# A fused attention and channel-mix kernel: a reworked head, and a tanh whose planned dependency is one half of its PSUM bank

## The chip, the cores and the metric

The kernel runs on one core of a Trainium2 chip. The core has TensorE (matmuls and, beside them, weight loads), VectorE (DVE), ScalarE (ACT), GpSimd (POOL) and SyncE (SP), each with a queue of its own that is worked in order, and 16 DMA engines. The metric is the device time of one execution in microseconds (us). The kernel before takes 528.45 us, the median of three runs (527.47 to 528.96).

## The reference, cut to what matters

```python
# q, k, v: [B, N, C] = [4, 6208, 256] float32; tau = 1.0
qn = q / (norm(q, axis=1) + 1e-6);  kn = k / (norm(k, axis=1) + 1e-6)
a  = softmax(kn.transpose(0, 2, 1) @ qn / tau)      # [B, 256, 256], over the last axis
x  = v @ a                                          # [B, N, 256]
x_prev = x shifted by one row along N, zeros first
xk = mu_k * x + (1 - mu_k) * x_prev;  xr = mu_r * x + (1 - mu_r) * x_prev
k  = maximum(xk @ w_k, 0)                           # w_k: [256, 1024]
v  = (k * k) @ w_v                                  # w_v: [1024, 256]
out = v / (1 + exp(-(xr @ w_r)))                    # w_r: [256, 256]
```

## The kernel before, in words

**Batches and blocks.** Each batch has 6208 = 12 x 512 + 64 rows. For each batch the kernel needs first a covariance of k with q over all rows and the norms of their columns, then a softmax that gives the 256 x 256 matrix A, and then works through the rows in blocks of 512 (the four rests of 64 rows make one block together, 49 blocks in all). While the blocks of one batch are worked, the covariance of the next is gathered, group by group (lines 615 to 665).

**One block.** The rows of v are turned so that rows lie along the free axis (DMA transposes from line 341, for the first five blocks transposes on TensorE at line 351, copied out of PSUM by DVE at line 353). x is A times the turned v (line 427) and is copied out of PSUM by ScalarE (437; for the first block half by DVE, 434). DVE makes the differences of neighbouring rows and the two mixes xk and xr (467, 475, 484). "Up" (513) multiplies xk with w_k in four pairs of 512-wide results in the PSUM tiles kT0 and kT1; ScalarE takes the relu (516) and DVE squares it (518). Then, for each of the block's four tiles of 128 rows, one of two PSUM banks vr0, vr1 is used: the **gate** (546) writes xr times w_r to the right half `V[:, D:]`, and four **down** steps (551), each of two matmuls, gather the product with w_v in the left half `V[:, :D]`. ScalarE takes the **tanh** (555) of the right half, and DVE (557) adds one, multiplies with the left half and writes the result tile. The bank of a tile is used again two tiles later.

**The head.** Batch 0 has nothing to lie beside. SP loads q and k in float32, 512 KB at a time, into a ring of ten tiles (280), DVE casts them to bf16 (291) into eight tiles for q (q0) and three for k (k0); ScalarE, for every second k DVE (297), squares them (300) into a ring of three tiles (s0). TensorE adds the covariance (313) and the column sums of the squares (306 for q into vr1, 319 for k into vr0). The short group 12 (64 rows) is loaded between groups 5 and 6 of k. Then come the q norms (lines 236 to 267, with a power on POOL at 239), a softmax chain over DVE, POOL and ScalarE (365 to 393), x, the mixes and the first up. Loads of v, of the weights and of the next batch's q and k are issued by POOL, and these DMAs cast to bf16 on their way (335, 673 to 681, 622).

**What sets the order.** All of this is given to a planner (`Plan`, lines 24 to 101). `add(engine, duration, key, function, reads, writes)` enters a step; the names in reads and writes are the planner's own and make its dependencies. `order()` plans each engine's steps: a step is ready when its predecessors end plus a fixed lag (0.3 us towards TensorE, 0.12 to ScalarE and DVE, 0.15 to POOL, 0.02 on the same engine), and of the ready steps that with the lowest key starts. The instructions are then emitted in the order of planned start, and that order is each engine's program order. The plan's times are not known to the chip: what an instruction waits for there is worked out anew by the framework, from the tiles that the emitted instructions touch, in the order in which they were emitted. A dependency given by `after=` alone exists in the plan only; before the change the loads of v and of the weights are held in this way behind the planned cast of k's group 10.

Of the kernel before, what the change touches and what calls it, by code (L numbers as in the profile page):

```python
# [113 lines left out]
def dve(n, mode=1):  # L114
    return 0.16 + n / 960 / mode
# [3 lines left out]
def kernel(  # L119
# [13 lines left out]
    nc = tc.nc  # L133
    B, N, C = q.shape
    D = C
# [18 lines left out]
    def ring(name, n, shape, dt=BF16):  # L154
        return [sbuf(f"{name}{i}", shape, dt) for i in range(n)]
# [9 lines left out]
    w_r = sbuf("w_r", [2, D])  # L165
    A = [sbuf(f"A{b}", [2, C]) for b in range(B)]

    NF, NQ0, NK0 = 10, 8, 3
    f32s = ring("f32s", NF, [S, C], F32)
    q0 = ring("q0", NQ0, [S, C])  # L170
    k0 = ring("k0", NK0, [S, C])
    s0 = ring("s0", 3, [S, C])
    sq = ring("sq", 2, [2, S, C])
    t1 = ring("t1", 2, [2, 2, C])
    t2 = ring("t2", 2, [2, C])
# [96 lines left out]
    for i, (tn, g, j0, j1) in enumerate(order0):  # L272
        key = H0 + i
        t = q if tn == "q" else k
        rows = P if g < NB else L
        fs = fslot % NF
        fslot += 1
        f = f32s[fs]
        n = j1 - j0
        add("SP", 0.45, key, lambda f=f, t=t, g=g, j0=j0, j1=j1, rows=rows: nc.sync.dma_start(  # L280
            f[:rows, j0:j1], src(t, 0, g)[:, j0:j1, :]), writes=[("f", fs)], size=rows * n * C * 4, name="ld0")
        if tn == "q":
            ci = g % NQ0
            cast, cres = q0[ci], ("q0", ci)
        else:
            ci = g % NK0
            cast, cres = k0[ci], ("k0", ci, j0)
        wr = [cres]
        if tn == "k" and j0 == 0:
            wr = [("k0", ci, 0), ("k0", ci, 2), ("k0", ci, 3)] if g != NB - 1 else [("k0", ci, 0)]  # L290
        add("DVE", dve(n * C, 2), key, lambda f=f, cast=cast, j0=j0, j1=j1, rows=rows: nc.vector.tensor_copy(
            cast[:rows, j0:j1], f[:rows, j0:j1]), reads=[("f", fs)], writes=wr, name="cast0")
        si = nsq % 3
        nsq += 1
        s2 = s0[si]
        if tn == "k" and g < NB - 1 and g % 2 == 1:
            add("DVE", dve(n * C, 2), key + 0.5, lambda s2=s2, cast=cast, j0=j0, j1=j1, rows=rows: nc.vector.tensor_tensor(
                s2[:rows, j0:j1], cast[:rows, j0:j1], cast[:rows, j0:j1], op=OP.mult), reads=[cres], writes=[("s0", si)], name="sq0")
        else:
            add("ACT", act(n * C), key, lambda s2=s2, f=f, j0=j0, j1=j1, rows=rows: nc.scalar.activation(  # L300
                s2[:rows, j0:j1], f[:rows, j0:j1], AF.Square), reads=[("f", fs)], writes=[("s0", si)], name="sq0")
        if tn == "q":
            for j in range(j0, j1):
                def go(s2=s2, j=j, rows=rows, st=(i == 0 and j == 0)):
                    for ih in range(2):
                        nc.tensor.matmul(vr[1][:, ih:ih + 1], s2[:rows, j, ih * P:(ih + 1) * P], ones[:rows, 0:1],
                                         start=st and ih == 0, stop=False, skip_group_check=True)
                add("PE", 0.13, key + 0.3, go, reads=[("s0", si)], writes=[("vr", 1)], name="nq0")
        else:
            for j in range(j0, j1):  # L310
                def go(ci=ci, g=g, j=j, rows=rows):
                    for ih in range(2):
                        nc.tensor.matmul(s_ps[:, ih, :], k0[ci][:rows, j, ih * P:(ih + 1) * P], q0[g % NQ0][:rows, j],
                                         start=g == 0 and j == 0 and ih == 0, stop=False, skip_group_check=True)
                add("PE", 2 * pe(C), key + 0.1, go, reads=[cres, ("q0", g % NQ0)], writes=[("s_ps",)], name="cov0")

                def go(s2=s2, j=j, rows=rows, st=(g == 0 and j == 0)):
                    for ih in range(2):
                        nc.tensor.matmul(vr[0][:, ih:ih + 1], s2[:rows, j, ih * P:(ih + 1) * P], ones[:rows, 0:1],
                                         start=st and ih == 0, stop=False, skip_group_check=True)  # L320
                add("PE", 0.16, key + 0.2, go, reads=[("s0", si)], writes=[("vr", 0)], name="nk0")
        if tn == "q" and g == NB:
            kq = key + 0.6
            add("DVE", dve(2), kq, lambda: nc.vector.tensor_copy(nrm[0][:, 0:2], vr[1][:, 0:2]),
                reads=[("vr", 1)], writes=[("nq", 0)], name="rq")
            inverse(0, kq, nrm[0], "nq", 0, 2, "rq")
            spread(0, kq, "rq")
# [17 lines left out]
    def v_turn_pe(n, key, pb, other=None):  # L345
        i, o = n % NV, n % NT
        tp = pb[0]

        def go():
            for j in range(2 * S):  # L350
                nc.tensor.transpose(tp[:, j * P:(j + 1) * P], v_bf[i][:, j // 2, (j % 2) * P:(j % 2 + 1) * P], ident)
        add("PE", 8 * 0.06, key, go, reads=[("v_bf", i)], writes=[pb[1]] + ([other] if other else []), name="turn v")
        add("DVE", dve(2 * M, 2), key + 0.1, lambda: nc.vector.tensor_copy(vT[o].rearrange("p a b -> p (a b)"), tp),
            reads=[pb[1]], writes=[("vT", o)], name="turn v")

# [50 lines left out]
    def x_stage(n, key):  # L406
# [11 lines left out]
        for ci, (c0, c1) in enumerate(cuts):  # L418
            for dh in range(2):
                kx = key + dh * (.3 * T if n else .01) + ci * .05  # L420

                dst = xp[:, c0:c1] if n else kT[0][:, dh, c0:c1]
                dres = ("xp",) if n else ("kT", 0, dh)

                def go(dh=dh, c0=c0, c1=c1, dst=dst):
                    for ih in range(2):
                        nc.tensor.matmul(dst, A[b][:, ih, dh * P:(dh + 1) * P],  # L427
                                         vT[o].rearrange("p (s h) q -> p h s q", h=2)[:, ih, c0 // P:c1 // P, :],
                                         start=ih == 0, stop=ih == 1)

                def both(go=go, kx=kx, w=c1 - c0, dh=dh, c0=c0, c1=c1, dst=dst, dres=dres):
                    add("PE", 2 * pe(w), kx, go, reads=[("A", b, 0), ("A", b, 1), ("vT", o)], writes=[dres], name="x")
                    if n == 0 and dh == 1:
                        add("DVE", dve(w), kx, lambda: nc.vector.tensor_copy(xR[:, dh, at + c0:at + c1], dst),
                            reads=[dres], writes=[("x", i, dh)], name="x evac")
                    else:
                        add("ACT", act(w), kx, lambda: nc.scalar.copy(xR[:, dh, at + c0:at + c1], dst),  # L437
                            reads=[dres], writes=[("x", i, dh)], name="x evac")
                unit(kx, both)

    def mix_stage(n, key):
# [93 lines left out]
    def down_tile(n, s, kd, last):  # L535
# [3 lines left out]
        def go():  # L539
# [4 lines left out]
            def gate():  # L544
                for dh in range(2):
                    nc.tensor.matmul(V[:, D:], xr[ri][:, dh, s * P:(s + 1) * P], w_r[:, dh, :], start=dh == 0, stop=dh == 1)  # L546
            add("PE", 2 * pe(D), kd, gate, reads=[("xr", ri), ("w_r",)], writes=[("vr", bk)], name="gate")
            for p in range(4):
                def dn(p=p):
                    for fh in (2 * p, 2 * p + 1):  # L550
                        nc.tensor.matmul(V[:, :D], kk[n % 2][:, fh, s * P:(s + 1) * P], w_v[:, fh, :], start=fh == 0, stop=fh == 7)  # L551
                c0 = (256 if s * P >= 256 else 0) if n == 0 else 0
                add("PE", 2 * pe(D), kd + .01 * p, dn, reads=[("kk", n % 2, p, c0), ("w_v",)], writes=[("vr", bk)], name="down")
            r = res[oi]
            add("ACT", act(D), kd + .3, lambda: nc.scalar.activation(r[:, s], V[:, D:], AF.Tanh, scale=0.5),  # L555
                reads=[("vr", bk)], writes=[("res", oi, s)], name="tanh")
            add("DVE", 0.15 + D / 960, kd + .4, lambda: nc.vector.scalar_tensor_tensor(  # L557
                r[:, s], r[:, s], 1.0, V[:, :D], op0=OP.add, op1=OP.mult), reads=[("vr", bk)], writes=[("res", oi, s)], name="out")
            if last:
# [53 lines left out]
    def cov_group(b, g, key, dk):  # L613
# [12 lines left out]
        def work():  # L626
# [28 lines left out]
            def go():  # L655
                for x in range(4):
                    nc.tensor.matmul(xp[:, x:x + 1], cols[x], ones[:rows, 0:1], start=x == 0, stop=x == 3,
                                     skip_group_check=True)
            add("PE", 0.3, kn, go, reads=[wres], writes=[("xp",)], name="norm")
            ai = b % 2  # L660
            if g == 0:
                add("DVE", dve(4), kn + .1, lambda: nc.vector.tensor_copy(acc[ai], xp[:, 0:4]), reads=[("xp",)], writes=[("acc", ai)], name="norm")
# [4 lines left out]
        unit(key, work)  # L667


    gate_w = [s for s in cast_done if s.name == "cast0"][-4:-3]  # L670
    gate_qk = gate_w
    v_load(0, KC - 2, after=gate_w)
    add("POOL", 0.75, KC - 1.9, lambda: nc.gpsimd.dma_start(w_k, moe_w_k.rearrange("(ko ki) f -> ki ko f", ki=P)),
        writes=[("w_k",)], size=D * DF * 4, name="ld w", after=gate_w)
# [13 lines left out]
    add("PE", 0.3, KC + .01, go, reads=[("mu_rows", 0), ("mu_rows", 1)], writes=[("vr", 1)], name="mu")  # L688
    add("DVE", dve(4), KC + .01, lambda: nc.vector.tensor_copy(mu, vr[1][:, 0:4]), reads=[("vr", 1)], writes=[("mu",)], name="mu")
    tps = [kT[1][:, 0, :].bitcast(BF16), kT[1][:, 1, :].bitcast(BF16)]  # L690
    v_turn_pe(0, KC + .02, (tps[0], ("kT", 1, 0)))
    v_turn_pe(1, KC + .5, (tps[1], ("kT", 1, 1)))

    NPE = 5
    for n in range(2, NPE):
# [34 lines left out]
        fn()  # L730
    seq = plan.order()
    tc_plan[:] = seq
    for s in seq:
        s.fn()


# [36 lines left out]
```

## Time and profile before

| what | value |
|---|---|
| median of three runs | 528.45 us |
| the profiled execution, its own time | 527.72 us |
| its span in the trace | 526.0 us |
| DVE busy | 417.8 us (79%) |
| ScalarE busy | 398.5 us (76%) |
| L551 down matmuls, 1552 of them | 273 ns each, one tile uses eight |
| L555 tanh, 194 of them | 387 ns each |
| L557 result on DVE, 194 of them | 417 ns each |
| L516 relu, 200 of them | 1001 ns each |
| L634 squares of the next batch on ScalarE, 39 of them | 1816 ns each |

The span is the time from the first to the last instruction that the profile shows; the rest of the execution's own time lies around it. Matmuls are pipelined, so two of 273 ns that follow each other at once are shown as 0.38 us together, and TensorE's busy time is that of overlapping instructions counted once. "PE" stands for TensorE's matmuls, "PEld" for its weight loads. In a list of instructions, x2 stands for two instructions merged into one line. A bracket at the end of a line holds the idle time of the engine before the instruction and what ended it.

### The profile page before, as it was taken

The page shows a single profiled execution, that of the slowest core. Times are in us where ns is not written, and L with a number is a line of the kernel's source. Part 1 is how long each engine was busy: PE and PEld are TensorE (multiplying, and loading weights), DVE is VectorE, ACT ScalarE, POOL GpSimd, SP SyncE. Part 2 cuts the span into 40 slices and gives each one's busy share as a digit, 9 for nine tenths or more (in the row PEclk, how much of TensorE's full clock was granted, in tenths as well). Part 3 has the DMA queues.
Part 4 walks back from the last instruction along what each step waited for, and adds up shares of the span by engine and source line. Part 5 has one row for each costly group of instructions (what it writes and reads, how often), then busy time and mean ns, then how long its engine had stood idle before and what let it go on. Part 6 is the DMA issues. An engine that isn't in the chain of part 4 may idle for free.

```text
span 526.0 us, 9943 instructions
## 1 busy us (share of the span) xinstructions
PE 491.1 (93%) x3707; PEld 342.7 (65%) x3761; DVE 417.8 (79%) x970; ACT 398.5 (76%) x573; POOL 88.7 (17%) x148
## 2 busy tenths in 40 slices
PE   1785999999899999999999999999999999999996
PEld 1563777756567767666667776666666666666674
DVE  4565997788879877798888778798888887878873
ACT  6543999788789978877898868877776787777763
POOL 0054433331123233211111210010010100000000
PEclk9998999999999999999999999999999999999999
DMA  8999999999999999998758854556465563413123
GB/s 333 402 312 206 205 187 203 197 203 206 212 191 133 205 188 161 210 215 128 127 106 145 147 90 92 126 102 145 97 99 143 105 143 81 121 40 102 41 81 100
DMA packets 113944, 83.23 MB, mean 158 GB/s; under 512 B 49572, under 2 KB 101352, under 8 KB 113896
## 3 DMA queue, kind: packets, MB, share of 16 engines
q0 software_dynamic: 38160, 33.01, 43.1%
q1 hardware_dynamic: 75736, 49.59, 36.5%
q8 instruction: 29, 0.48, 0.4%
q14 instruction: 19, 0.16, 0.1%
HBM read 78.71 MB, written 25.43 MB: 198 GB/s over the span
## 4 chain that ended last, share of the span: by engine, by line
PE 77%; DVE 7%; DMA 7%; issue 4%; ACT 3%; POOL 2%; SPq 0%; ACTq 0%; POOLq 0%
PE vr L551 28%; PE kT L513 28%; PE vr L546 7%; PE xp L427 6%; PE s_ps L650 6%; DMA f32s<-in_q_dram 3%; ACT kr L516 2%; DMA f32s<-in_k_dram 2%; DMA vT<-v_bf 2%; DVE kk L518 2%; DVE dm L475 1%; DVE res L557 1%; DVE dl L467 1%; DVE xk L484 1%; POOL v_bf L335 1%
## 5 line engine op out<-in xcount | busy, mean ns | idle before, releaser
L551 PE MATMUL vr<-w_v,kk 128*128 128x256 bf16 x1552 | 251.3, 273 | 1.0
L516 ACT ACTIVATE kr<-kT 128x1024 bf16<-128x1024 f32 (+1 forms) x200 | 198.6, 1001 | 53.2 <-PE kT L513 48.3
L513 PE MATMUL kT<-xk,w_k 128*128 128x512 bf16 (+1 forms) x746 | 213.4, 372 | 7.5 <-DVE xk L484 4.5
L551 PEld LDWEIGHTS <-kk 128*128 128x128 bf16 x1552 | 149.2, 98 | 83.8 <-issue 0.4
L518 DVE TENSOR_TENSOR kk<-kr 128x1024 bf16<-128x1024 bf16 (+1 forms) x200 | 134.7, 674 | 49.2 <-ACT kr L516 47.2
L555 ACT ACTIVATE res<-vr 128x256 f32<-128x256 f32 x194 | 74.1, 387 | 37.6 <-PE vr L551 35.1
L513 PEld LDWEIGHTS <-w_k 128*128 128x128 bf16 x800 | 77.6, 98 | 33.3 <-issue 5.0
L557 DVE SCALAR_TENSOR_TENSOR res<-res,vr 128x256 f32<-128x256 f32 x194 | 80.4, 417 | 18.2 <-ACT res L555 17.2
L546 PE MATMUL vr<-w_r,xr 128*128 128x256 bf16 x388 | 72.7, 272 | 2.5 <-DVE res L557 2.2
L634 ACT ACTIVATE sq<-f32s 128x2048 bf16<-128x2048 bf16 (+1 forms) x39 | 70.8, 1816 | 0.0
L335 POOL DMA_DIRECT2D v_bf<-in_v_dram x48 | 36.8, 766 | 197.4 <-DMA vT<-v_bf 170.3
L475 DVE TENSOR_SCALAR dm<-dl,mu 128x512 bf16<-128x512 bf16 (+1 forms) x200 | 62.4, 349 | 0.6
L437 ACT CAST xR<-xp 128x512 bf16<-128x512 f32 x94 | 55.3, 589 | 7.7 <-PE xp L427 7.2
L427 PE MATMUL xp<-vT,A 128*128 128x512 bf16 x188 | 56.9, 385 | 0.1
L546 PEld LDWEIGHTS <-xr 128*128 128x128 bf16 x388 | 37.7, 98 | 19.7 <-issue 3.8
L650 PE MATMUL s_ps<-f32s 128*128 128x256 bf16 (+1 forms) x294 | 48.8, 272 | 0.1
L467 DVE TENSOR_TENSOR dl<-xR 128x1024 bf16<-128x1024 bf16 (+1 forms) x49 | 33.1, 677 | 9.2 <-ACT xR L437 9.2
L300 ACT ACTIVATE s<-f32s 128x1024 bf16<-128x1024 f32 (+3 forms) x23 | 21.1, 926 | 18.3 <-DMA f32s<-in_q_dram 9.1
L622 POOL DMA_DIRECT2D f32s<-in_q_dram x39 | 21.1, 541 | 74.0 <-ACT res L555 15.1
L484 DVE TENSOR_TENSOR xk<-dm,xR 128x1024 bf16<-128x1024 bf16 (+1 forms) x49 | 33.2, 678 | 0.3
L484 DVE TENSOR_TENSOR xr<-dm,xR 128x1024 bf16<-128x1024 bf16 (+1 forms) x49 | 33.2, 677 | 0.3
L650 PEld LDWEIGHTS <-f32s 128*128 128x128 bf16 (+1 forms) x294 | 28.0, 97 | 4.7 <-issue 0.6
(68 smaller groups left out, 237.5 us busy)
## 6 DMA issues: line engine op xcount, KB each, us to landing
out_dram<-res SPq DMA_DIRECT2D x47, 512.0 KB, 3.7
v_bf<-in_v_dram POOLq DMA_DIRECT2D x48, 256.0 KB, 6.6
f32s<-in_q_dram POOLq DMA_DIRECT2D x36, 256.0 KB, 9.6
f32s<-in_k_dram POOLq DMA_DIRECT2D x36, 256.0 KB, 9.8
f32s<-in_q_dram SPq DMA_DIRECT2D x12, 512.0 KB, 7.7
f32s<-in_k_dram SPq DMA_DIRECT2D x11, 512.0 KB, 9.5
vT<-v_bf SPq DMA_TRANSPOSE x43, 3.9
w_k<-in_moe_w_k_dram POOLq DMA_DIRECT2D x1, 512.0 KB, 8.6
```

Of the source, the lines that this page charges most:

```text
L427: nc.tensor.matmul(dst, A[b][:, ih, dh * P:(dh + 1) * P], vT[o].rearrange("p (s h) q -> p h s q", h=2)[:, ih, c0 // P:c1 // P, :], start=i ...
L475: unit(km, lambda col=col, dh=dh, c0=c0, c1=c1, km=km, w=w: add("DVE", dve(w, 4), km, lambda: nc.vector.tensor_scalar_mul(dm[di][:, dh, c0 ...
L484: nc.vector.tensor_tensor(o[which][:, :, c0:c1], dm[di][:, :, c0:c1], xR[:, :, at + c0:at + c1], op=OP.add)
L513: nc.tensor.matmul(kT[bk][:, x, :w], w_k[:, dh, fh * P:(fh + 1) * P], xk[n % 2][:, dh, c0:c1], start=dh == 0, stop=dh == 1)
L516: add("ACT", act(2 * w), ku + .1, lambda: nc.scalar.activation(kr[kri][:, :, :w], kT[bk][:, :, :w], AF.Relu, scale=0.5 ** 0.5), reads=[("k ...
L518: add("DVE", dve(2 * w, 2), ku + .2, lambda: nc.vector.tensor_tensor(kk[n % 2][:, 2 * p:2 * p + 2, c0:c1], kr[kri][:, :, :w], kr[kri][:, : ...
L546: nc.tensor.matmul(V[:, D:], xr[ri][:, dh, s * P:(s + 1) * P], w_r[:, dh, :], start=dh == 0, stop=dh == 1)
L551: nc.tensor.matmul(V[:, :D], kk[n % 2][:, fh, s * P:(s + 1) * P], w_v[:, fh, :], start=fh == 0, stop=fh == 7)
L555: add("ACT", act(D), kd + .3, lambda: nc.scalar.activation(r[:, s], V[:, D:], AF.Tanh, scale=0.5), reads=[("vr", bk)], writes=[("res", oi, ...
L557: add("DVE", 0.15 + D / 960, kd + .4, lambda: nc.vector.scalar_tensor_tensor(r[:, s], r[:, s], 1.0, V[:, :D], op0=OP.add, op1=OP.mult), re ...
L634: add("ACT", act(w), key, lambda: nc.scalar.activation(Q[:rows, :, :n], G[:rows, :, :n], AF.Square), reads=both, writes=[("sq", si)], name ...
L650: nc.tensor.matmul(s_ps[:, ih, :], G[:rows, 1, s, ih * P:(ih + 1) * P], G[:rows, 0, s, :], start=g == 0 and s == 0 and ih == 0, stop=g == ...
```

## The change

The change edits two places.

In the **head**: the ring for squares s0 grows from three to six tiles and that for k from three to five. The planned costs of the norm steps on TensorE fall (0.13 and 0.16 to 0.06, in later batches 0.3 to 0.15). The loads that POOL issues are no longer held in the plan only: a small copy on POOL reads the cast of k's group 9, and all loads are planned after it; since it is an instruction of POOL's queue, what is emitted behind it on POOL runs behind it. The first two turned blocks of v are copied out of PSUM by ScalarE and no longer by DVE, with other keys. The planner's resource for the first block's x is split into two column halves, so that the plan no longer holds the second quarter's matmuls behind the first one's copy. Last, "fillers": between the last norm step of k and the first gate, matmuls with no use are emitted into the right half of vr1, as many as fill 0.8 of each gap that the plan shows on TensorE.

In the **tiles of every block**: the gate writes a planner's resource of its own, `("vr", bk, "g")`, and the tanh reads that alone and is entered ahead of the down steps. So in the plan the tanh depends on the gate and no longer on the four down steps. The gate in turn depends on the last down step of the tile before in its bank, and no longer on DVE's read of that tile.

```diff
-    NF, NQ0, NK0 = 10, 8, 3
+    NF, NQ0, NK0 = 10, 8, 5
-    s0 = ring("s0", 3, [S, C])
+    s0 = ring("s0", 6, [S, C])
...
-        si = nsq % 3
+        si = nsq % 6
...
-                add("PE", 0.13, key + 0.3, go, reads=[("s0", si)], writes=[("vr", 1)], name="nq0")
+                add("PE", 0.06, key + 0.3, go, reads=[("s0", si)], writes=[("vr", 1)], name="nq0")
...
-                add("PE", 0.16, key + 0.2, go, reads=[("s0", si)], writes=[("vr", 0)], name="nk0")
+                add("PE", 0.06, key + 0.2, go, reads=[("s0", si)], writes=[("vr", 0)], name="nk0")
...
+        if n < 2:
+            add("ACT", 1.03, key + 0.1, lambda: nc.scalar.copy(vT[o].rearrange("p a b -> p (a b)"), tp),
+                reads=[pb[1]], writes=[("vT", o)], name="turn v")
+            return
...
-                dres = ("xp",) if n else ("kT", 0, dh)
+                dres = [("xp",)] if n else [("kT", 0, dh), ("kT", 0, dh, c0)]
...
-                    add("PE", 2 * pe(w), kx, go, reads=[("A", b, 0), ("A", b, 1), ("vT", o)], writes=[dres], name="x")
+                    add("PE", 2 * pe(w), kx, go, reads=[("A", b, 0), ("A", b, 1), ("vT", o)] + (dres[:1] if n == 0 else []), writes=dres[-1:], name="x")
...
-            add("PE", 2 * pe(D), kd, gate, reads=[("xr", ri), ("w_r",)], writes=[("vr", bk)], name="gate")
+            add("PE", 2 * pe(D), kd, gate, reads=[("xr", ri), ("w_r",), ("down", bk)], writes=[("vr", bk, "g")], name="gate")
+            r = res[oi]
+            add("ACT", act(D), kd + .3, lambda: nc.scalar.activation(r[:, s], V[:, D:], AF.Tanh, scale=0.5),
+                reads=[("vr", bk, "g")], writes=[("res", oi, s)], name="tanh")
             for p in range(4):
...
-                add("PE", 2 * pe(D), kd + .01 * p, dn, reads=[("kk", n % 2, p, c0), ("w_v",)], writes=[("vr", bk)], name="down")
-            r = res[oi]
-            add("ACT", act(D), kd + .3, lambda: nc.scalar.activation(r[:, s], V[:, D:], AF.Tanh, scale=0.5),
-                reads=[("vr", bk)], writes=[("res", oi, s)], name="tanh")
+                add("PE", 2 * pe(D), kd + .01 * p, dn, reads=[("kk", n % 2, p, c0), ("w_v",)], writes=[("vr", bk), ("down", bk)], name="down")
...
-    gate_w = [s for s in cast_done if s.name == "cast0"][-4:-3]
-    gate_qk = gate_w
+    gate = sbuf("gate", [1])
+    gate_qk = gate_w = [add("POOL", 0.3, KC - 3, lambda: nc.gpsimd.tensor_copy(gate, k0[(NB - 3) % NK0][:, 0, 0:1]),
+                            reads=[("k0", (NB - 3) % NK0, 0)], writes=[("gate",)], name="gate")]
...
-    v_turn_pe(0, KC + .02, (tps[0], ("kT", 1, 0)))
-    v_turn_pe(1, KC + .5, (tps[1], ("kT", 1, 1)))
+    v_turn_pe(0, KC - .02, (tps[0], ("kT", 1, 0)))
+    v_turn_pe(1, KC + .36, (tps[1], ("kT", 1, 1)))
...
+    fill_from = max(s.start for s in seq if s.name == "nk0")
+    fill_to = min(s.start for s in seq if s.name == "gate" and s.eng == "PE")
+    free = None
     for s in seq:
+        if s.eng == "PE":
+            if free is not None and fill_from < s.start <= fill_to:
+                for _ in range(int(0.8 * (s.start - free) / pe(C))):
+                    nc.tensor.matmul(vr[1][:, C:], ident, q0[0][:, 0], start=True, stop=True)
+            free = s.start + s.dur
         s.fn()
```

More of the change, by code (lines that the diff above doesn't have):

```diff
@@ L431, in both @@
                 def both(go=go, kx=kx, w=c1 - c0, dh=dh, c0=c0, c1=c1, dst=dst, dres=dres):
-                    add("PE", 2 * pe(w), kx, go, reads=[("A", b, 0), ("A", b, 1), ("vT", o)], writes=[dres], name="x")
+                    add("PE", 2 * pe(w), kx, go, reads=[("A", b, 0), ("A", b, 1), ("vT", o)] + (dres[:1] if n == 0 else []), writes=dres[-1:], name="x")
                     if n == 0 and dh == 1:
                         add("DVE", dve(w), kx, lambda: nc.vector.tensor_copy(xR[:, dh, at + c0:at + c1], dst),
-                            reads=[dres], writes=[("x", i, dh)], name="x evac")
+                            reads=dres, writes=[("x", i, dh)], name="x evac")
                     else:
                         add("ACT", act(w), kx, lambda: nc.scalar.copy(xR[:, dh, at + c0:at + c1], dst),
-                            reads=[dres], writes=[("x", i, dh)], name="x evac")
+                            reads=dres, writes=[("x", i, dh)], name="x evac")
                 unit(kx, both)
@@ L658, in go @@
                                      skip_group_check=True)
-            add("PE", 0.3, kn, go, reads=[wres], writes=[("xp",)], name="norm")
+            add("PE", 0.15, kn, go, reads=[wres], writes=[("xp",)], name="norm")
             ai = b % 2
```

## The prediction

> **What bounds the kernel now.** I read the page first, then the busy time by windows, then the list of waits, then the timeline of the head (0 to 62 us) and of a stretch in the middle.
>
> ```profile
> span 526.0 us, 9943 instructions
> PE 491.1 (93%) x3707; PEld 342.7 (65%) x3761; DVE 417.8 (79%) x970; ACT 398.5 (76%) x573; POOL 88.7 (17%) x148
> PE   1785999999899999999999999999999999999996
> ```
>
> TensorE is busy in 93% of the span, and its row of tenths is 9 from the fifth slice on. The windows say it more sharply:
>
> ```profile
> 40.00:50.00 10.00, 6.10 (x54) 3.55 (x51) 4.52 (x14) 3.15 (x10) 5.20 (x9) 0.83 1.27 205
> 200.00:300.00 100.00, 98.74 (x730) 68.24 (x738) 83.28 (x197) 83.97 (x120) 18.73 (x30) 1.00 0.89 157
> 400.00:500.00 100.00, 99.17 (x676) 67.21 (x690) 83.07 (x188) 74.34 (x118) 3.70 (x6) 1.00 0.40 94
> ```
>
> The first number after the length is TensorE's busy time: 1.3 us idle between 200 and 300, 0.8 between 400 and 500. So TensorE sets the end; a microsecond it loses anywhere after 62 us is lost for the whole. The head (to about 57 us) is a chain of another kind: loads, then TensorE at half rate, then the softmax chain.
>
> **The tanh (the large part).** Three rows of the waits show how the program guards the banks of vr:
>
> ```profile
> ACT res L555 <- PE vr L551: 35.1, 53, 2.2
> ACT s L300 <- PE vr L319: 7.4, 4, 2.9
> PE vr L546 <- DVE res L557: 2.2, 5, 0.7
> ```
>
> L555 is the tanh, which reads only the gate's half of the bank; yet 53 times ScalarE sat idle until a down matmul (L551, the other half) had ended. The third row is the reverse case, and decides: the gate (L546) writes the right half and waits for the DVE step (L557) that reads the left half. So whatever the planner notes of halves, the built program orders all accesses to a bank as they are emitted, a TensorE write behind a read of the other half too.
>
> The emission order is the planned start. Before, the tanh depended on the last of four down steps. After, it is ready 0.12 us after the gate in the plan, and is planned as soon as ScalarE is free; every down step emitted later than it must then wait for it, on TensorE, with all of TensorE's queue behind. The middle of the run shows what that meets:
>
> ```profile
> 301.01 1.05 ACT L516 ACTIVATE kr<-kT 128x1024 bf16<-128x1024 f32 x1
> 301.42 0.38 PE L546 MATMUL vr<-w_r,xr 128*128 128x256 bf16 x2
> 301.86 0.38 PE L551 MATMUL vr<-w_v,kk 128*128 128x256 bf16 x2
> ...
> 302.30 0.38 PE L551 MATMUL vr<-w_v,kk 128*128 128x256 bf16 x2
> ...
> 302.73 0.38 PE L551 MATMUL vr<-w_v,kk 128*128 128x256 bf16 x2
> ...
> 303.17 0.38 PE L551 MATMUL vr<-w_v,kk 128*128 128x256 bf16 x2
> ...
> 303.59 0.38 ACT L555 ACTIVATE res<-vr 128x256 f32<-128x256 f32 x1 [1.53 <-PE vr L551]
> ```
>
> Columns: start, duration, engine, line. The gate starts at 301.42, the four down steps follow 0.44 apart with covariance matmuls between, and ScalarE is free from 302.06. The new tanh goes there, behind the down step of 301.86 and before that of 302.30.
>
> Price of one such tanh: the step before it ends 0.38 after its start; the tanh starts 0.04 later (303.17 + 0.38 = 303.55, tanh at 303.59), takes 0.38, and the release of TensorE takes about 0.05 (at 47.84 a DVE step ends, at 47.88 L427 starts). Sum 0.85 from one down step to the next, instead of 0.44: a stall of 0.41. I went through the timeline tile by tile in this way, ScalarE's other work left where it is. In 149 of 194 tiles ScalarE comes free between the gate and the last down step; the stall there is 0.41 us in the mean (mean spacing of down steps 0.47). 149 x 0.41 = **61 us**. The other 45 tiles keep the tanh behind the downs, at nothing.
>
> Bounds: below, half the tiles (97) at 0.25 us, as the planner's ScalarE is fuller than the chip's and as other TensorE work may sit beside the wait: 24 us. Above, all 194 at 0.61 (down steps back to back, 0.24 apart, as at 306.64 with 0.60 for four matmuls): 118 us. The five existing waits of L546 (2.2 us, 0.44 each) are the nearest row of one bank wait on TensorE, and they agree with 0.41. Gains of the earlier tanh: DVE's step L557 waited 17.2 us for it, but DVE is not the bound. In the last two tiles the two tanhs behind the last down (0.82 us at 521.60) come off the end: about -0.4 us.
>
> The Trainium skill, "PSUM — Partial Sum Buffer", section "PSUM bank collisions raise a hardware error", says that two engines on one bank and quadrant collide even at different columns and that PSUM is to be guarded by bank. By a rule of addresses this edit would cost nothing and gain the -0.4; by the page's rule the stalls stand.
>
> **The head, step by step.**
> *Six tiles for squares, five for k.* ScalarE waited 7.4 us for the k-norm matmuls (L319), since three s tiles were full; the cast of k at 32.18 waited for L313. The last piece of k is issued at 29.4 and takes 7.8 us to land, so 37.2; the last covariance starts at 40.8, so TensorE is late, not the loads. Four covariance and four norm steps take 2.05 us per group while matmuls start 0.21 apart, and 1.07 us after 36.2 where they start 0.11 apart. From 29.35 on 7.3 groups are open (5 to 11 and the short one). If TensorE, no longer interrupted, speeds up 3.4 us earlier (the low stretch of the clock later, 46.5 to 49.9, is as long): 3.5 us slow are 1.7 groups, 5.6 x 1.07 follow, end at 38.8. If not, 6.9 us slow are 3.4 groups, end at 40.4. Now it is 41.0. I take -1.5 us, between the two; bounds -3.6 (the loads) and 0.
> *Cast loads behind a copy of k on POOL.* The first load of v was issued at 30.77; now POOL waits for the cast of group 9, issued at 24.9 and, with the 9 us of its kind, landed near 33.9. Behind it queue all of POOL's issues: v, w_k, w_r, w_v, q and k of the next batch, later the softmax's pow. Head loads land up to 1 us earlier (33.9 plus two groups at 1.27, the pitch of the early issues, is 36.4). The first v (6.6 to 9.7 us from issue to landing) comes at 41 to 44, needed turned for x at about 43. I take 0: the transfers keep their total, and the lower figure suffices; bounds -1 and +3.
> *Turned v on ScalarE.* DVE's two copies (L353, 0.68 and 0.67) delay the norm copy by 0.5 (42.0 to 42.52) and the second A by 0.5 (45.25 to 45.76): -1.0 us. ScalarE's copy (nearest row: 0.59 for 512 elements, 1.02 for 1024) lies in ScalarE's idle 2.4 us before the exponentials; if not, it costs its 1.0: bounds -1.0 and +1.0.
> *x by quarter banks.* The plan no longer holds the second quarter, but the bank order above does (L427 at 47.88 waited for L434): 0.
> *Fillers.* TensorE's mean clock is 0.63 and 0.52 in the windows 46 to 48 and 48 to 50. Kept warm, eight x matmuls on the path start 0.11 instead of 0.21 apart: -0.6. The filler number follows planned gaps at 0.8; an overrun holds the chain a few tenths: bounds -1 and +1.
> Lower planned costs of norm steps only reorder: 0.
>
> The skill's "TensorE: Matmul & The Clock Gate", Part 1, gives about 3.4 us of activity for full clock and the same idle for half. It agrees with that record, but its section "A second HAM failure mode: psum-queue depth-cycling" says that frequent short idles around PSUM banks throttle too. By that the tanh stalls would cost clock as well, which no row here shows.
>
> Head: -1.5 + 0 - 1.0 + 0 - 0.6 = -3.1 us.
>
> **Sum.** The profiled execution took 527.72 us (span 526.0 plus 1.7 outside), 0.1% under the median 528.45. 527.7 + 61 - 0.4 - 3.1 = 585.2, on the median's scale 0.7 more: **586 us**.
>
> **Rivals.**
> *The tanh stays behind the downs.* ScalarE's planned queue is so full that tanhs come after the last down step, as 45 tiles already do; or the bank wait is not built for this pair. Then only the head counts: 528.4 - 3.5 = 524.9, faster. For: ScalarE is 84% busy at 200 to 300. Against: 53 tanhs ended an idle time of ScalarE. It decides below about 9 tiles with a stall (3.5 / 0.41). Chance 0.10.
> *The head gives nothing and few tanhs stall* (under 4 us together): within 0.3% of 528.4. Chance 0.03.
> *The stalls feed on themselves.* A tanh that waits in ScalarE's strict order also holds the relu behind it, so squares and the next downs come late; every tile pays the upper price: 528.4 + 118 - 3.5 = 643. If the clock falls to half in stretches as well, it is more: at 50 to 60 us TensorE was busy 8.1 of 10 us with clock 1.00, which speaks against that. Chance 0.12.
> *Main case,* 550 to 620 around 586: 0.75.
>
> **How the numbers follow.** The predicted time is the main case. The range leaves out the faster side (0.13 with the unchanged case) and some of the upper rival: 548 (24 us of stalls, less 4) to 635, short of the upper rival's 643. 0.3%, 1.6 us, is about what a measurement here can tell from no change. Slower: 0.75 + 0.12 = 0.87; same 0.03; faster 0.10.
>
> **What would show it.** Right: a wait of L551 for the tanh line on ScalarE near 150 times and some 60 us in all, TensorE idle about 12% in 200 to 300, ScalarE's wait for L551 much below 35.1. The head: first full up matmuls about 3 us earlier, clock 1.00 from 40 to 50. Wrong: tanhs that start only after the fourth down step, or TensorE still 98% busy there; then the first rival holds. A first v landing after 42 would show the POOL hold.

## The result and the profile after

| kernel | median (range), us | ratio to before, 95% interval |
|---|---|---|
| before | 528.7 | |
| changed | 557.8 (555.0 to 560.6) | 1.0555 (1.0499 to 1.0612) |

The changed kernel is 29 us slower, half of the loss that was forecast (586 us, range 548 to 635). The profiled execution took 557.28 us with a span of 555.5, 29.5 more than before. The page of the changed kernel:

```profile
span 555.5 us, 10169 instructions
PE 516.6 (93%) x3815; PEld 348.4 (63%) x3815; DVE 416.9 (75%) x968; ACT 403.8 (73%) x575; POOL 90.2 (16%) x149
L558 PE MATMUL vr<-w_v,kk 128*128 128x256 bf16 x1552 | 259.6, 272 | 15.1 <-ACT res L553 11.8
L558 PEld LDWEIGHTS <-kk 128*128 128x128 bf16 x1552 | 149.5, 97 | 112.7 <-issue 39.2
L561 DVE SCALAR_TENSOR_TENSOR res<-res,vr 128x256 f32<-128x256 f32 x194 | 81.0, 418 | 74.0 <-PE vr L550 32.1
```

The lines have moved: down is L558, gate L550, tanh L553, the result step L561. TensorE's share stays 93% and its busy time *grows* by 25.5 us with the same products. The 54 fillers (L745) add some 6 us of that, and up to 12 come from records: of the 800 up matmuls before, the trace holds 746. The rest is that a busy time of matmuls hides short stalls: a matmul that is not followed at once shows its full 272 ns, while one that is followed at once adds only about 0.11 us. The weight loads do not hide them. Their idle time in front of downs that is put to "issue" (no released wait of their own; they stand behind the matmul that waits) went from 0.4 to 39.2 us, and the tanh's line appears as a releaser of downs. The waits of the changed kernel:

```profile
ACT res L553 <- PE vr L558: 45.5, 98, 0.9
PEld L558 <- issue: 39.2, 110, 0.9
DVE res L561 <- PE vr L550: 32.1, 35, 1.8
...
PE vr L558 <- ACT res L553: 11.8, 42, 0.8
```

The second half of each step is in its timeline:

```profile
301.43 1.04 PE L558 MATMUL vr<-w_v,kk 128*128 128x256 bf16 x8
...
302.30 0.38 PE L654 MATMUL s_ps<-f32s 128*128 128x256 bf16 x2
...
302.50 0.38 ACT L553 ACTIVATE res<-vr 128x256 f32<-128x256 f32 x1 [0.23 <-PE vr L558]
...
302.94 0.38 PE L558 MATMUL vr<-w_v,kk 128*128 128x256 bf16 x2 [0.25 <-ACT res L553]
```

The last of the eight down matmuls ends at 302.47, the tanh starts 0.03 later, ends at 302.88, and the next down starts 0.06 behind it, though TensorE could have gone on at 302.52.

To add such gaps up, I take for every matmul after 60 us the time to the next start, less its own streaming time (0.11 us for 256 columns, 0.216 for 512), and book what is over 0.06 us to the line that starts late; such sums are called **gaps** below. Before: 4.4 us in front of downs (22 times), 4.3 of gates. Changed: **33.9 in front of downs (122 times, 0.28 each)**, 2.1 of gates. Of the 33.9, 30.7 us (103 times, 0.30 each) end with the tanh and 2.5 with DVE's result step. Of the 4.4 before, only 0.3 us end with a wait that the trace shows; 18 of the 22 are of some 0.2 us, as long as one of the 54 up matmuls without a record. The growth of 30 to 33 us in front of downs is nearly all of the loss. (Gaps of up matmuls are not compared, for the same reason.) By stage, the first gate of the changed kernel comes 0.6 us later than before, that of block 16 (225 us) 4.5, of block 30 12.8, of block 47 27.6: not the head, but a steady loss, largest after 225 us.

### The profile page after: what moved, and what is told of

It reads as the page before. It is cut to its first block, busy times and chain, and to the rows that moved or that the text cites. A ratio compares the mean times of both kernels' runs of the same rounds, so it can differ in the third digit from the quotient of the medians.

```text
span 555.5 us, 10169 instructions
## 1 busy us (share of the span) xinstructions
PE 516.6 (93%) x3815; PEld 348.4 (63%) x3815; DVE 416.9 (75%) x968; ACT 403.8 (73%) x575; POOL 90.2 (16%) x149
## 4 chain that ended last, share of the span: by engine, by line
PE 77%; DMA 10%; ACT 5%; DVE 4%; issue 2%; POOL 1%; SPq 0%; DVEq 0%; POOLq 0%; ACTq 0%
PE vr L558 29%; PE kT L517 28%; PE vr L550 7%; PE xp L431 6%; PE s_ps L654 5%; DMA f32s<-in_k_dram 4%; ACT res L553 3%; DMA out_dram<-res 3%; DMA v_bf<-in_v_dram 2%; DVE res L561 1%; DMA vT<-v_bf 1%; DMA f32s<-in_q_dram 1%; DVE kk L522 1%; ACT sq L638 1%; PE xp L661 0%
## 5 line engine op out<-in xcount | busy, mean ns | idle before, releaser
L558 PE MATMUL vr<-w_v,kk 128*128 128x256 bf16 x1552 | 259.6, 272 | 15.1 <-ACT res L553 11.8
L520 ACT ACTIVATE kr<-kT 128x1024 bf16<-128x1024 f32 (+1 forms) x200 | 196.4, 998 | 47.5 <-PE kT L517 45.3
L558 PEld LDWEIGHTS <-kk 128*128 128x128 bf16 x1552 | 149.5, 97 | 112.7 <-issue 39.2
L522 DVE TENSOR_TENSOR kk<-kr 128x1024 bf16<-128x1024 bf16 (+1 forms) x200 | 133.3, 670 | 24.9 <-ACT kr L520 24.5
L561 DVE SCALAR_TENSOR_TENSOR res<-res,vr 128x256 f32<-128x256 f32 x194 | 81.0, 418 | 74.0 <-PE vr L550 32.1
L553 ACT ACTIVATE res<-vr 128x256 f32<-128x256 f32 x194 | 71.7, 385 | 63.3 <-PE vr L558 45.5
L550 PE MATMUL vr<-w_r,xr 128*128 128x256 bf16 x388 | 71.5, 272 | 0.5 <-ACT res L553 0.4
L654 PE MATMUL s_ps<-f32s 128*128 128x256 bf16 (+1 forms) x294 | 50.7, 272 | 0.0
L550 PEld LDWEIGHTS <-xr 128*128 128x128 bf16 x388 | 37.4, 97 | 9.1 <-issue 1.6
```

What stands on the lines that cost most here:

```text
L520: add("ACT", act(2 * w), ku + .1, lambda: nc.scalar.activation(kr[kri][:, :, :w], kT[bk][:, :, :w], AF.Relu, scale=0.5 ** 0.5), reads=[("k ...
L522: add("DVE", dve(2 * w, 2), ku + .2, lambda: nc.vector.tensor_tensor(kk[n % 2][:, 2 * p:2 * p + 2, c0:c1], kr[kri][:, :, :w], kr[kri][:, : ...
L654: nc.tensor.matmul(s_ps[:, ih, :], G[:rows, 1, s, ih * P:(ih + 1) * P], G[:rows, 0, s, :], start=g == 0 and s == 0 and ih == 0, stop=g == ...
```

## The experiments

All are compared with runs of the kernel before in the same jobs (528.3 to 528.8 us).

**The two edits apart.** e1 is the kernel before with the tile hunks of the diff, e2 the changed kernel without them.

> The kernel before with only the edit of the tiles (gate's own resource, tanh entered ahead of the downs). Bank theory (a down step emitted behind a tanh waits for it on TensorE): the whole loss is here. The trace of the changed kernel shows 33.9 us of gaps of TensorE in front of its down line against 4.4 before, so 528.5 + 29 = 557 us, between 550 and 565. Rival, the head loses the time (its first up starts 0.8 us later and its second turned v holds TensorE for 2.5 us): then this kernel stays under 535 us.

> The changed kernel with the tiles as before, so the head's edit alone. Bank theory: the head is worth little either way; in the changed kernel the first gate came 0.6 us later than before, so 529 us, between 525 and 532. Rival, the head loses the time: about 555 us.

Measured: e1 560.6 us, ratio 1.0606 (1.0585 to 1.0626), gaps in front of downs 37.3 us (126 times). e2 533.7 us, 1.0102 (1.0087 to 1.0117). So the loss is the tiles'. But the head is not nearly neutral, and e2 ends above the range expected: the head costs 5.4 us alone, and 32.4 + 5.4 is more than the 29 of both. In e2 the head does what it should in the head: up starts at 48.9 us (51.2 before), with the clock at 1.00. It loses the lead at one place (the second fence is a window: its length, then TensorE's busy time; the granted clock is third from the end):

```profile
104.57 9.25 SPq L341 DMA_TRANSPOSE vT<-v_bf  x1
...
125.35 1.03 PE L431 MATMUL xp<-vT,A 128*128 128x512 bf16 x2 [6.50 <-DMA vT<-v_bf]
```

```profile
126.00:128.00 2.00, 2.00 (x10) 1.33 (x9) 0.31 (x1) 0.72 (x2) 0.05 (x1) 0.50 1.12 241
```

TensorE waits 6.5 us for a turned v, whose transpose, issued at 104.57, landed 20.7 us later. In the wait the granted clock falls to half, from 121.4 to 128.2 us, so for 2.9 us after it the matmuls run at half rate too. Against before, block 5 starts 1.5 us earlier and block 6 7.4 us later; from there on the distance stays between 3.6 and 9.3 (5.6 at the end). In the changed kernel, whose TensorE is slower, that wait is absent; this fits a sum that does not add up.

**The tanh behind the downs, the gate still freed; and the wait told to the planner.** e3 and e4 are the changed kernel with

```diff
# e3: the tanh entered after the down steps
+                reads=[("vr", bk, "g"), ("vr", bk)], writes=[("res", oi, s)], name="tanh")
# e4: the first down step also writes what the tanh reads
- ... writes=[("vr", bk), ("down", bk)], name="down")
+ ... writes=[("vr", bk), ("down", bk)] + ([("vr", bk, "g")] if p == 0 else []), name="down")
```

> The changed kernel, gate with its own resource, but the tanh entered behind the four down steps and made to depend on them. Bank theory: no down step waits for a tanh, so within 3 us of the kernel with the head alone (526 to 533 us). Rival, the freed gate does the harm (it now runs ahead of the result step of the tile before in its bank, and that step waits for it: 32.1 us of DVE waiting for the gate line in the changed kernel): then it stays above 545 us.

> The changed kernel, with the wait told to the planner: the first down step also depends on the tanh, which so stands ahead of all four downs in every tile. Bank theory: the wait is the same on the chip, but the planner puts other matmuls between gate and first down step, and the loss mostly goes: 527 to 535 us, with fewer than 40 waits of the down line for the tanh. Rival, an early tanh costs by its place alone (ScalarE's order, DVE's waits): 545 us or more.

Measured: e3 550.2 us (1.0393, 1.0355 to 1.0430), e4 541.4 (1.0237, 1.0213 to 1.0260). e3 goes to the rival: no down waits for a tanh, and it is still 16.5 us over e2. Its gaps stand in front of gates (17.7 us, 30 times) and downs (13.2, 61); 15.1 us of the first and 9.4 of the second end with DVE's result step. Its waits:

```profile
DVE res L561 <- PE vr L550: 34.8, 49, 1.9
...
PEld L550 <- issue: 18.1, 29, 3.9
...
PE vr L550 <- DVE res L561: 10.5, 14, 3.7
```

The gate's planned start no longer knows that this step reads the bank; in the built program the gate still waits for it. So the freed gate has a price of its own. e4 lies between the two ranges: the downs' gaps fall from 33.9 to 11.5 us, of which 7.7 (26 times) still end with the tanh, less than I had expected to be saved.

**Tanh and gate apart, on the kernel before.**

```diff
# e7: tanh ahead of the downs, gate as before
- ... writes=[("vr", bk)], name="gate")
+ ... writes=[("vr", bk), ("vr", bk, "g")], name="gate")
+ ... reads=[("vr", bk, "g")], writes=[("res", oi, s)], name="tanh")    # entered here, no longer behind the downs
# e8: gate as in the change, tanh entered behind the downs, reads ("vr", bk, "g"), ("vr", bk)
```

> The kernel before, with the tanh entered ahead of the downs and tied to the gate's half, but the gate still planned behind the result step of the tile before in its bank. This is the case that the prediction priced: gates directly ahead of their downs, 160 tanhs emitted ahead of a down step, 0.41 us each. Bank theory with that price: 528 + 60 = 588, between 565 and 600 us. Rival, the early tanh is cheaper than that and part of the changed kernel's loss belongs to the freed gate: 540 to 560 us.

> The kernel before, with the gate freed of the result step and the tanh behind its downs. With the head edited, this cost 16.5 us over the head alone, 17.7 us of it in gaps of TensorE in front of gates that wait for the result step of their bank. If that belongs to the gate, 540 to 546 us. If it came with the head's late loads, under 535 us.

Measured: e7 **556.2 us** (1.0517, 1.0504 to 1.0531), e8 **543.7** (1.0276, 1.0262 to 1.0291). Each alone costs much (27.4 and 14.9 us); together on this head 32.4. e7 falls into its rival's range, e8 into that of its own theory. e7's gaps: 36.0 us in front of downs, 125 times (34.3 us and 115 of them end with the tanh), 1.6 of gates. Its waits:

```profile
ACT res L549 <- PE vr L554: 54.8, 113, 1.3
...
PEld L554 <- issue: 42.1, 117, 0.6
...
PE vr L554 <- ACT res L549: 13.0, 46, 0.5
```

So the mechanism is the predicted one and the price is not: 0.30 us for each tanh that holds a down, where 0.41 was forecast.

**The same plan, the tanh emitted late.** e9 and e10 take the plan of e7 and of the changed kernel, and emit each tanh right behind its last down step.

```diff
...
+        if s in late and late[s] not in emitted:   # late[tanh] = last down step
+            held[late[s]] = s
+            continue
         s.fn()
+        emitted.add(s)
+        if s in held:
+            held[s].fn()
+            emitted.add(held[s])
```

> The plan of the kernel with the tanh alone edited, instruction for instruction, but each tanh is emitted right behind the last down step of its tile and no longer where it was planned. Bank theory: nothing is left for a down step to wait for, so nearly all of the 27.4 us go: 528 to 534 us. Rival, the plan's order of the other steps carries the loss: 545 us or more.

> The changed kernel itself, with each tanh emitted right behind its last down step. What is left then is the head (5.4 us alone) and the freed gate (15 us alone), what goes is the wait of the downs for the tanh. Bank theory with a share for the gate: 540 to 552 us, gaps of TensorE in front of downs under 15 us and in front of gates over 8. If the freed gate is harmless in the changed kernel: 530 to 536 us. If the waits for the tanh cost nothing: 557 us.

Measured: e9 543.7 us (1.0280, 1.0265 to 1.0295), e10 565.8 (1.0712, 1.0693 to 1.0731). In e9 the gaps in front of downs fall from 36.0 to 0.8 us: those waits were for the tanh, as nothing differs but the place where it is emitted. But only 12.5 of 27.4 us come back, between the two ranges expected, since gaps in front of gates rise from 1.6 to 13.1, all of which end with DVE's result step. Its waits:

```profile
DVE res L558 <- ACT res L550: 56.9, 78, 2.1
...
PEld L547 <- issue: 13.2, 24, 1.6
PE vr L547 <- DVE res L558: 8.5, 17, 1.5
```

The plan counted on an early tanh, so that only the result step lies between the last down and the next gate of the bank; with the tanh behind the downs both lie there. e10 refutes all that I expected: it is 8 us slower than the changed kernel. A freed gate is planned directly behind the last down of its bank, and the late tanh now stands in front of it: 36.2 us of gaps, 75 times, in front of gates, 28.1 of them ended by the tanh.

```profile
PEld L551 <- issue: 37.7, 75, 1.4
...
PE vr L551 <- ACT res L554: 19.1, 54, 1.4
```

In the changed kernel the early tanh thus spares its freed gates a wait, which fits that the two tile edits cost less together than the sum of each alone (32.4 against 27.4 + 14.9).

**The head's loss.** e5 is e2 with the planned dependency on k's group 10 in place of the POOL copy; e6 is e2 with the second block of v loaded ahead of w_k; e11 is e5, and e12 the kernel before, with `NPE = 9` for `NPE = 5` (nine blocks of v turned on TensorE, not five).

> The head alone, less the POOL copy that holds the cast loads (they start behind a planned step only, as before, near 31 us and not 35.6). Hold theory: the head's 5.4 us of loss are the 6.7 us in which TensorE waits near 125 us for a turned v, whose loads run 4.6 us later behind DMA engines that are full from 35 to 200 us; so that wait goes, the earlier first up (48.9 against 51.2 us) stays, and the time is 524 to 528 us. Rival, another part of the head (copies on ScalarE, fillers, five k tiles) changes the planner's order for the worse: 531 us or more.

> The head alone, with the hold, but the second block of v loaded ahead of w_k, so that TensorE's second turn need not wait for it (2.5 us in the changed kernel). Hold theory: the head gets no worse, the wait near 125 us stays or grows, since the stream of loads is as late as before: 531 to 535 us. Rival, the head loses its time in the head, behind the late second v: 527 to 530 us.

> The head without the hold, tiles as before, with nine blocks of v turned on TensorE instead of five (blocks 5 to 8 no longer need a DMA transpose). Theory of the full DMA engines: the waits for turned v near 118 to 142 us go, TensorE pays about 1.8 us for 32 transposes, and the 3 us that this head lost there come back in part: 526 to 530 us. Rival, the loss there is the planner's order: 531 us or more.

> The kernel before with nine blocks of v turned on TensorE instead of five, nothing else. Theory of the full DMA engines: the kernel before has no wait of TensorE for a turned v over 1 us, so it has nothing to win there and pays about 1.8 us for 32 transposes: 528 to 531 us, and the 525.9 us of the head without the hold with nine turns belong to both edits together. Rival, the turns alone are the gain: 524 to 527 us.

Measured: e5 531.2 us (1.0061, 1.0042 to 1.0080); e6 537.4 (1.0166, 1.0152 to 1.0179); **e11 525.9 (0.9957, 0.9942 to 0.9972)**; e12 528.2 (0.9986, 0.9975 to 0.9997). The hold is 2 to 3 of the head's 5.4 us, less than expected: e5 ends just inside its rival's range, and TensorE still waits 2.5 us for a turned v (at 141.8). e6 missed its range on the slow side: the second copy of a turned v stands ahead of the exponentials in ScalarE's queue and waits for that v, so the second half of A starts at 46.60 us and not at 43.80, and there are still 5.1 us of wait at 128.9, with the clock at 0.50 from 125 to 130. e11 takes away what remains. The windows 100 to 130 and 130 to 200 of e5, then of e11 (busy TensorE first, the DMA share last but one):

```profile
100.00:130.00 30.00, 26.01 (x185) 16.73 (x186) 24.08 (x55) 23.48 (x36) 8.82 (x15) 1.00 1.21 200
130.00:200.00 70.00, 65.10 (x482) 45.11 (x489) 56.18 (x139) 54.70 (x77) 15.22 (x25) 1.00 1.13 182
```

```profile
100.00:130.00 30.00, 29.78 (x227) 19.82 (x225) 26.43 (x62) 24.02 (x35) 6.20 (x10) 1.00 1.37 164
130.00:200.00 70.00, 69.02 (x519) 48.01 (x518) 57.73 (x138) 58.75 (x81) 17.12 (x28) 1.00 1.13 190
```

The DMA engines are full in this stretch (share over 1; in e5 a transpose lands up to 21.5 us after its issue where the median is 4.1), so a head that hands TensorE its work earlier meets the loads and transposes sooner. With four DMA transposes fewer TensorE's wait for a turned v goes, and the head's lead is kept: 2.9 us (0.4%) faster than the kernel before. On the kernel before, which has no such wait over a microsecond, the same edit moves the time by 0.1%. Two limits: the DMA share stays over 1 in e11 and is 1.21 from 100 to 130 us in the kernel before too, so what e11 takes away is TensorE's dependence on late transposes; that the full engines make them late is argued, not shown. And of the 5.3 us between e5 and e11 the waits for a turned v are only some 2.7; gaps in front of gates fall as well, from 7.5 to 4.4, and why is open.

## Why the prediction was right and where it was off

- **The mechanism of the tanh: right.** Downs emitted behind a tanh wait for it on TensorE, though the two touch different halves of the bank. Shown by e7 (36.0 us of gaps there) and e9 (0.8 when the tanh is emitted behind them). The latencies were right too: 0.04 us to the tanh, 0.05 to the down, in the median over the tiles of e7.
- **Its size: 61 us forecast, 30.7 found in the changed kernel and 34.3 in e7.** The count of early tanhs was close: 149 forecast, and by the order of emission 160 in e7 and 180 in the changed kernel stand ahead of a down step. But only 115 and 103 of them hold one, for 0.30 us each. What was mis-sized is the term "mean spacing of down steps 0.47". Adding up the streaming times from the down before the tanh to the one behind it gives 0.78 in the mean in the changed kernel and 0.74 in e7. Taken off 0.85 tile by tile, and never below nothing, this leaves 0.22 and 0.23; the traces show 0.21 and 0.23 in the mean of these tiles. The forecast took its spacing over all downs. A tanh falls more often into a wide gap, beside a pair of up matmuls (two of 0.216), than into a short one: weighted by their length, the spacings of the kernel before give a stall of 0.29 and not 0.37. And the new plan sets the downs wider apart (0.58 in the mean in e7, 0.50 before, by streaming times).
- **The freed gate: not priced.** The prediction took gates to stand directly ahead of their downs and spoke of the tanh alone. In the changed kernel 56 tiles have the tanh emitted ahead of all four downs, and some 2.5 us lie between the gate and the first down; these wait 0.09 us in the mean. And 77 result steps are emitted behind the next gate of their bank, so DVE waits 32.1 us for gates. e8 and e3 show that the freed gate costs 14.9 and 16.5 us where the tanh is late. That the loss of the changed kernel (29 us) is near that of the tanh alone (27.4) is thus chance: the gate and the head, 14.9 and 5.4 us alone, mostly vanish beside it.
- **The head: -3.1 forecast, +5.4 found alone.** The steps inside the head were about right: A comes 2.3 us earlier in the profile of the changed kernel (43.94 against 46.24), and in e2 up starts 2.3 earlier. Wrong was "I take 0" for the hold of the loads, and that a lead of the head reaches the end: the forecast read DMA's share only in the head. The hold is 2 to 3 us (e5 against e2), and nine turns on TensorE take away the rest (e11). The -0.6 for the fillers was not earned in the profiled execution of the changed kernel: its second v landed so late that TensorE waits 2.5 us for it, the clock falls to half from 46.1 to 49.5 us, as it does in the kernel before from 46.5 to 49.9, and the first gate comes 0.6 us late. e2's profile shows a wait of 0.4 us at that place and the clock at 1.00. The wait and the clock in the changed kernel:

```profile
46.55 1.03 PE L351 MATMUL kT<-ident,v_bf 128*128 128x128 bf16 x8 [2.50 <-DMA v_bf<-in_v_dram]
```

```profile
46.00:48.00 2.00, 1.45 (x11) 1.28 (x12) 0.00 (x0) 0.38 (x1) 0.98 (x2) 0.51 1.45 199
```

- **x by quarter banks, forecast at 0:** no run parts it. The reason given, that the bank order still holds the second quarter, did not hold: all eight matmuls now run in a row, since they are emitted ahead of the copies, and the wait has moved to the copies, where ScalarE's start 1.54 us late, behind DVE's.

```profile
47.38 1.91 PE L431 MATMUL kT<-vT,A 128*128 128x256 bf16 x8
...
50.17 0.65 ACT L441 CAST xR<-kT 128x256 bf16<-128x256 f32 x2 [1.54 <-DVE xR L438]
```

- **The rivals.** The tanh did not stay behind the downs (14 tiles of 194), and the stalls did not feed on themselves: from 200 to 500 us the granted clock is 1.00 in every window of 50 us. What the prediction cites from the Trainium skill's page "TensorE: Matmul & The Clock Gate", section "A second HAM failure mode: psum-queue depth-cycling", on frequent short idles did not show here, at 122 gaps of 0.28 us.
- **The signs named ahead:** most did not come in the changed kernel. From 200 to 300 us TensorE is idle 3%, not 12%. ScalarE's wait for downs rose from 35.1 to 45.5 us where it was to fall: a tanh emitted between two downs waits for the one before it. Up starts at 52.0 us, 0.8 later than before and not 3 earlier, and the clock from 40 to 50 us is 0.83. The first v was there by 40.7; the second came at 46.5.

What stays open: how much of e4's 7.7 us over e2 is the freed gate and how much the planner's lag of 0.3 us; no run parts them.

## What to carry to other kernels

A planner's dependency may only be finer than the guard that the built program uses if the emission order still suits that guard: here the plan knew halves of a bank, the program whole tiles in emission order, and a read and a write that never touch the same bytes cost 27 us in line on the bounding engine. Price such a wait by the work that stands between the two instructions it parts, at the place where the third one lands, not by the mean. And before speeding up a head, read what TensorE waits for behind it: the gain counted only after that wait was gone.

## What the runs showed of the hardware

TensorE's share of busy time was 93% in both kernels, with 29 us between them; the idle time of weight loads told them apart (0.4 and 39.2 us in front of downs). A copy of one column on POOL took 0.70 us, near the 0.72 of a power there. A wait of 6.5 us on TensorE was followed by 2.9 us at half the clock (e2); of two waits of 2.5 us, one went with half the clock (the changed kernel, 46.1 to 49.5 us) and one did not (e5, at 141.8).
